# Softmax denominators of the first two attentions: key sums from three sources in one TensorE accumulation

## Chip, cores and metric

The kernel runs on one core of a Trainium2 chip. The metric is device time in microseconds (us) of one execution; the number to predict is the median over the timed runs of the changed kernel.

## The reference, cut to what matters

Three layers follow one another: an attention with capped scores, a dense feed-forward layer with squared ReLU, and a layer of eight experts with routing. The change touches only the sum of the exponentials over the keys, the denominator of the softmax, in the attention.

```python
def _attn_ref(q, k, v, cap):          # 4 batches, 12 heads, 448 tokens, head size 64
    scale = 1.0 / np.sqrt(q.shape[-1])
    scores = scale * np.matmul(q, k.transpose(0, 1, 3, 2))
    scores = cap * np.tanh(scores / cap)
    scores = scores - np.max(scores, axis=-1, keepdims=True)
    attn = np.exp(scores)
    attn = attn / (np.sum(attn, axis=-1, keepdims=True) + 1e-09)
    return np.matmul(attn, v).astype(np.float32)
def _moe_ref(x, w_in, w_out):         # 1792 x 768, width 2048
    h = x @ w_in
    r = np.maximum(h, 0.0)
    g = r * r
    return (g @ w_out).astype(np.float32)
...
```

The weights `w_in` and `w_out` arrive as 64-bit floating point numbers and are decoded on the chip; the kernel splits operands into a high and a low part to multiply at float32 accuracy.

## The kernel before, in words

Work is done batch by batch (b = 0 to 3). `attention(b)` handles the 12 heads as six pairs `hp` of two heads each. The 448 keys are cut into three chunks of 128 (c = 0, 1, 2) and a rest of 64. `scores(hp, c)` multiplies keys by queries for both heads of a pair (L239), the two heads standing side by side; for c = 3 the rests of both heads are packed into one tile, head 0 in rows 0 to 63 and head 1 in rows 64 to 127 (L241). ScalarE (ACT) then applies tanh (L243) and exp (L244), which gives the tiles `p` with keys on rows and queries on columns. `pv` multiplies them by the values into a tile `U` (L263). `norm(hp)` forms the denominators: the chunks have been added up elementwise in a tile `z`, and a matmul with a 128x64 block of ones sums over the 128 rows and spreads the sum over the 64 rows of each head (L269). Then L271 adds a small constant, L272 takes the reciprocal, and L274 multiplies `U` by it, which gives `x`.

The elementwise additions are: L250, chunk 0 plus chunk 1; L252, plus chunk 2; L256, twice, plus the packed rest, one half of the rows for each head. They run on VectorE (DVE) for b = 0 and on GpSimd (POOL) for b = 1 to 3.

```python
adder = nc.vector if b == 0 else nc.gpsimd
...
elif c == 2:
    adder.tensor_add(zs[hp], zs[hp], p)
elif c == KB:
    for s in range(2):
        half = slice(s * 64, s * 64 + 64)
        adder.tensor_add(zs[hp][half, s], zs[hp][half, s], p[half, 0])
```

`hidden(b)` is the first product of the feed-forward layer (L404 to L406, in the rows `acc<-xh,wh`, `acc<-xl,wh`, `acc<-xh,wl`), `output(b)` the second (L461 to L463, `acc<-g,...`). It needs all six `x` of its batch, split by L320 (ACT) and L321 (DVE). For b = 0 the weights are also decoded, on DVE (L333, L334, L335, tile `wf`), and split into a high part on ACT (L361) and a low part on DVE or POOL (L362); later batches read them back from a cache. `merge` interleaves the generators by the costs that they yield: `attention(0)` runs first alone, then `hidden(0)` with `attention(1)`, then `output(0)` and `hidden(1)` with `attention(2)`, and so on. Each engine has its own list of instructions and works through it in order; for b below 2 a scheduler chose that order, from b = 2 on TensorE's order is that of `merge`.

PSUM is held by three pools of two buffers each: `big` (scores), `acc` (feed-forward) and `aux` (`U` and `z` in turn). With two `aux` buffers, the next `U` takes the buffer of the last `z`, free after L271, and the next `z` takes that of the last `U`, free after L274. So the matmul of one `norm` waits for L274 of the `norm` before it.

Of the kernel before, what the change touches and what calls it, by code (L numbers as in the profile page):

```python
# [9 lines left out]
F32 = mybir.dt.float32  # L10
# [9 lines left out]
NB, NH, S, DH = 4, 12, 448, 64  # L20
# [7 lines left out]
KB = S // 128  # L28
# [16 lines left out]
AHEAD = 12  # L45
PLAIN = 4
EARLY = 6
WB = 4
START, MASK, VOTE, REST, GATHER, LIST = (7.7, 8.0), (1.85, 3.4), (1.0, 2.6), (0.86, 2.2), (11.0, 12.4), (6.0, 10.0)

# [35 lines left out]
class Kernel:  # L86
# [96 lines left out]
    def setup(self):  # L183
        nc, keep = self.nc, self.keep
        capt = keep.tile([128, 1], F32, name="capt")
        nc.sync.dma_start(capt, bass.AP(tensor=self.capv.tensor, offset=self.capv.offset, ap=[[0, 128], [1, 1]]))
        self.capt = capt
        self.ones = keep.tile([128, DH], F32, name="ones")
        nc.vector.memset(self.ones, 1.0)
        self.isc = keep.tile([128, 1], F32, name="isc")  # L190
        nc.vector.reciprocal(self.isc, capt)
        nc.vector.tensor_scalar(self.isc, self.isc, DH ** -0.5, None, op0=OP.mult)
        nab = keep.tile([128, 1], F32, name="nab")
        nc.vector.scalar_tensor_tensor(nab, capt, -1.0, capt, op0=OP.mult, op1=OP.min)
        self.eps = keep.tile([128, 1], F32, name="eps")
        nc.scalar.activation(self.eps, nab, AF.Exp)
        nc.vector.tensor_scalar(self.eps, self.eps, 1e-9, None, op0=OP.mult)
        self.L = keep.tile([128, TC, NE], F32, name="L")
        self.cache = {}
        self.wtile = {}  # L200
        self.seq, self.at = [], {}
        for b, m in ((0, "i"), (0, "o"), (1, "i"), (1, "o"), (2, "i"), (3, "i"), (3, "o"), (2, "o")):
            self.at[b, m] = len(self.seq)
            self.seq += [(b, m, j) for j in range(NF if m == "i" else ND * OB)]
        self.G = {}
        self.loaded = self.ready = 0
        self.x_t = {}
        self.tail = []
        self.exps, self.norms = [], []
        self.mark = None  # L210

    def attention(self, b):

        nc, ap = self.nc, self.ap
        qk, P, vt, zs, U = {}, {}, {}, {}, {}
        adder = nc.vector if b == 0 else nc.gpsimd

        def load(hp):
            qk[hp] = t = ap.tile([128, QK], F32, name="qk", bufs=2)
            if b + hp == 0:  # L220
                for half, q in ((0, nc.sync), (1, nc.scalar)):
                    q.dma_start(t[half * 64:half * 64 + 64], self.q_k[b, hp, half * 64:half * 64 + 64])
            else:
                nc.sync.dma_start(t, self.q_k[b, hp])

        def load_v(hp):
            vt[hp] = ap.tile([128, KB + 1, 2 * DH], F32, name="v", bufs=3)
            nc.sync.dma_start(vt[hp], self.v[b, hp])

        def scores(hp, c):  # L230

            t = qk[hp]
            n = 2 if c < KB else 1
            k, q = t[:, c * 128:(c + 1) * 128], t[:, QK - S:]
            ps = self.psum.tile([128, 2, 512], F32, name="big")
            if c < KB:
                for s in range(2):
                    rows = slice(s * 64, s * 64 + 64)
                    nc.tensor.matmul(ps[:, s, :S], k[rows], q[rows], start=True, stop=True)  # L239
            else:  # L240
                nc.tensor.matmul(ps[:, 0, :S], k, q, start=True, stop=True)  # L241
            p = ap.tile([128, n, S], F32, name=f"p{n}", bufs=(2, 5)[n - 1])
            nc.scalar.activation(p, ps[:, :n, :S], AF.Tanh, scale=self.isc)  # L243
            e = nc.scalar.activation(p, p, AF.Exp, scale=self.capt)  # L244
            if b == 0:
                self.exps.append(e)
            P[hp, c] = p
            if c == 1:
                zs[hp] = z = ap.tile([128, 2, S], F32, name="z", bufs=2)
                adder.tensor_add(z, P[hp, 0], p)  # L250
            elif c == 2:
                adder.tensor_add(zs[hp], zs[hp], p)  # L252
            elif c == KB:
                for s in range(2):
                    half = slice(s * 64, s * 64 + 64)
                    adder.tensor_add(zs[hp][half, s], zs[hp][half, s], p[half, 0])  # L256

        def pv(hp, c0, c1):
            if c0 == 0:
                U[hp] = self.psum.tile([128, S], F32, name="aux")  # L260
            for c in range(c0, c1):
                for s in range(2):
                    nc.tensor.matmul(U[hp][s * 64:s * 64 + 64], vt[hp][:, c, s * 64:s * 64 + 64], P[hp, c][:, s if c < KB else 0],  # L263
                                     start=(c == 0), stop=(c == KB), skip_group_check=True)

        def norm(hp):
            z = self.psum.tile([128, S], F32, name="aux")
            for s in range(2):
                nc.tensor.matmul(z[s * 64:s * 64 + 64], self.ones, zs[hp][:, s], start=True, stop=True)  # L269
            d = zs[hp][:, 0]  # L270
            (nc.vector.tensor_scalar(d, z, self.eps, None, op0=OP.add) if b == 0 else nc.scalar.activation(d, z, AF.Identity, bias=self.eps))  # L271
            nc.vector.reciprocal(d, d)  # L272
            x = self.xq.tile([128, S], F32, name="x")
            m = nc.vector.tensor_mul(x, U.pop(hp), d)  # L274
            if b == 0:
                self.norms.append(m)
            if b == NB - 1:
                self.mark = m
            self.x_t[b, hp] = x

        load(0)
        load(1)
        load_v(0)
        whole = b > 1
        for hp in range(HP + 1):
            if hp < HP:
                if hp + 1 < HP:
                    load_v(hp + 1)
                scores(hp, 0)
                if not whole:  # L290
                    yield 0.8
                scores(hp, 1)
                if not whole:
                    yield 0.8
            if hp:
                pv(hp - 1, 0, 2)
                if not whole:
                    yield 1.6
                pv(hp - 1, 2, 4)
                if not whole:  # L300
                    yield 1.6
                norm(hp - 1)
            if hp or whole:
                yield (4.4 if hp else 1.6) if whole else 0.8
            if hp < HP:
                scores(hp, 2)
                if not whole:
                    yield 0.8
                scores(hp, 3)
                if hp + 2 < HP:  # L310
                    load(hp + 2)
                yield 2.6 if whole else 0.6
# [28 lines left out]
    def load_weights(self, n):  # L341
# [5 lines left out]
        if b == 0:  # L347
            wf = self.wts.tile([128, DM], F32, name="wf", bufs=3)
            with self.after(self.norms, WAIT[0], n):
                self.decode(wf, (self.wi if m == "i" else self.wo)[j], w)  # L350
            self.wtile[n] = (wf, w, nc.gpsimd if n % 6 else nc.vector, self.wts, WB)
        else:
            self.wtile[n] = pair = [self.wts.tile([128, DM], F32R, name=name, bufs=WB) for name in ("wh", "wl")]
            for t, c in zip(pair, self.cache[m, j]):
# [463 lines left out]
    def load_experts(self, n):  # L818
        nc = self.nc
        while self.eloaded < min(n + 1 + AHEAD, len(self.eseq)) and self.eseq[self.eloaded][0] in self.full:  # L820
# [9 lines left out]
            plain = kk < PLAIN and mm == 1  # L830
            pool, bufs = (self.ep, 4) if self.esplit % 8 < 4 else (self.wts, WB)
            self.esplit += not plain
# [20 lines left out]
    def expert(self, k):  # L853
# [5 lines left out]
        def part(j, d0, d1):  # L859
            if d0 == 0:  # L860
                W[j] = [t.rearrange("p (d f) -> p d f", d=ND) for t in self.expert_weights(k, 1, j)]
                if k == 0 and 2 <= j < EARLY:
                    if j % 2 == 0:
# [27 lines left out]
        if k == 0:  # L891
            for i in range(EARLY):
                p = part(i, 0, DA)
# [8 lines left out]
        for group in groups:  # L902
            for j in group:
                yield from part(j, DA if k == 0 and j < EARLY else 0, ND)
            for j in group:
# [97 lines left out]
```

## Time and profile before

| what | value |
|---|---|
| median of three timed runs (lowest, highest) | 1053.39 us (1051.45, 1054.56) |
| the profiled execution's own time | 1056.75 us |
| its span, first to last instruction | 1055.0 us |
| TensorE (PE) busy | 1026.5 us, 97% |
| VectorE (DVE) busy | 602.5 us, 57% |
| ScalarE (ACT) busy | 468.1 us, 44% |
| GpSimd (POOL) busy | 244.7 us, 23% |

The busy share is a mean over stages that differ. VectorE is busy nearly all the time in the first 250 us (decoding of weights) and much less later, so the first quarter of the span has to be read by itself. A float32 matmul shows as two records in the trace, so a row "x4" of the attention's matmuls is two matmuls, one for each head of a pair.

### The profile page before, as it was taken

How to read it: one execution, taken by the hardware profiler on the slowest of the kernel's cores; microseconds unless marked ns; L12 is line 12 of the kernel's file. 1: busy time of each engine (PE TensorE's matmuls, PEld its weight loads, DVE VectorE, ACT ScalarE, POOL GpSimd, SP SyncE). 2: the span in 40 equal slices, each digit the busy share in tenths (PEclk: the TensorE clock that was granted, in tenths of full speed). 3: DMA queues.
4: the chain of work that ended last, by engine and by line, in shares of the span. 5: the costliest groups of instructions: out<-in, count | busy, mean ns of one | idle time of the engine just before them, and what ended most of it. 6: DMA issues, size and time to landing. Idle time of an engine off the chain costs nothing.

```text
span 1055.0 us, 15657 instructions
## 1 busy us (share of the span) xinstructions
PE 1026.5 (97%) x5690; PEld 815.2 (77%) x5690; DVE 602.5 (57%) x1148; ACT 468.1 (44%) x725; POOL 244.7 (23%) x181
## 2 busy tenths in 40 slices
PE   6989999999999999999999999999999999999997
PEld 1335665777677777777888788888899999999997
DVE  5997999999122255555411234534647348677552
ACT  5867686654465543365544110100323224445542
POOL 0117776665221222222000100001220201021000
PEclk9999999999999999999999999999999999999999
DMA  8653877899655579988687268667567358567530
GB/s 280 233 169 130 261 257 264 247 324 323 247 181 189 175 256 336 364 308 307 236 303 253 80 197 276 204 193 243 167 226 259 113 178 265 189 200 250 180 119 27
DMA packets 102494, 237.60 MB, mean 225 GB/s; under 512 B 11088, under 2 KB 21872, under 8 KB 102416
## 3 DMA queue, kind: packets, MB, share of 16 engines
q1 hardware_dynamic: 87776, 219.65, 61.5%
q0 software_dynamic: 3424, 11.19, 3.6%
q10 hardware_dynamic: 11216, 5.75, 2.0%
q8 instruction: 45, 0.74, 0.3%
q14 instruction: 33, 0.27, 0.1%
HBM read 194.08 MB, written 42.47 MB: 224 GB/s over the span
## 4 chain that ended last, share of the span: by engine, by line
PE 71%; issue 12%; DVE 10%; DMA 3%; ACT 1%; POOL 1%; SPq 0%; POOLq 0%; ACTq 0%; DVEq 0%
PE big L939 8%; PE acc L404 7%; PE acc L405 6%; PE acc L406 6%; PE acc L461 6%; PE acc L871 6%; PE acc L462 6%; PE acc L463 6%; PE aux L263 4%; PE big L239 3%; DVE wf L334 3%; DVE wf L333 2%; PE acc L878 2%; PE aux L676 2%; PE aux L269 1%
## 5 line engine op out<-in xcount | busy, mean ns | idle before, releaser
L461 PE MATMUL acc<-g,wh 128*128 128x448 f32 x384 | 149.5, 389 | 0.0
L404 PE MATMUL acc<-xh,wh 128*128 128x448 f32 x384 | 145.9, 382 | 0.7 <-ACT r L411 0.7
L405 PE MATMUL acc<-xl,wh 128*128 128x448 f32 x384 | 140.8, 367 | 0.9 <-DVE xl L321 0.9
L462 PE MATMUL acc<-g,wh 128*128 128x448 f32 x384 | 140.1, 365 | 0.0
L463 PE MATMUL acc<-g,wl 128*128 128x448 f32 x384 | 139.6, 364 | 0.0
L406 PE MATMUL acc<-xh,wl 128*128 128x448 f32 x384 | 139.5, 363 | 0.0
L939 PE MATMUL big<-wh,g 128*112 128x384 f32 x512 | 118.5, 343 | 0.0
L243 ACT ACTIVATE p<-big,isc 128x896 f32<-128x896 f32 x96 | 85.8, 908 | 43.3 <-PE big L239 43.3
L272 DVE RECIPROCAL z<-z 128x448 f32<-128x448 f32 x24 | 70.8, 2949 | 57.4 <-ACT z L271 57.4
L416 DVE TENSOR_TENSOR g<-r,g 128x448 fp32r<-128x448 f32 x58 | 42.7, 738 | 104.1 <-ACT g L415 103.8
L404 PEld LDWEIGHTS acc<-xh,wh 128*128 128x128 f32 x384 | 71.6, 187 | 34.3 <-issue 15.6
L244 ACT ACTIVATE p<-p,capt 128x896 f32<-128x896 f32 x96 | 89.4, 948 | 1.7
L783 POOL DMA_INDIRECT xg<-x,idx x32 | 31.6, 987 | 246.6 <-PE aux L676 129.4
L939 PEld LDWEIGHTS big<-wh,g 128*112 128x112 f32 x512 | 86.7, 175 | 0.7
L461 PEld LDWEIGHTS acc<-g,wh 128*128 128x128 f32 x384 | 73.2, 191 | 11.7 <-issue 5.6
L263 PE MATMUL aux<-p,v 128*64 128x448 f32 x384 | 81.1, 549 | 0.3 <-DVE z L271 0.3
L405 PEld LDWEIGHTS acc<-xl,wh 128*128 128x128 f32 x384 | 72.1, 188 | 9.9 <-issue 2.4
L239 PE MATMUL big<-qk 64*128 64x448 f32 x288 | 73.4, 600 | 6.5 <-DMA qk<-qk 6.2
L411 ACT ACTIVATE r<-acc 128x448 f32<-128x448 f32 x64 | 34.8, 543 | 99.1 <-PE acc L406 87.6
L462 PEld LDWEIGHTS acc<-g,wh 128*128 128x128 f32 x384 | 72.4, 189 | 6.3 <-issue 2.2
L463 PEld LDWEIGHTS acc<-g,wl 128*128 128x128 f32 x384 | 72.0, 187 | 6.7 <-issue 0.7
L406 PEld LDWEIGHTS acc<-xh,wl 128*128 128x128 f32 x384 | 72.0, 188 | 6.7 <-issue 0.8
(179 smaller groups left out, 1802.6 us busy)
## 6 DMA issues: line engine op xcount, KB each, us to landing
g<-w SPq DMA_DIRECT2D x62, 384.0 KB
wh<-wih SPq DMA_DIRECT2D x48, 384.0 KB
wl<-wil SPq DMA_DIRECT2D x48, 384.0 KB
wh<-woh SPq DMA_DIRECT2D x72, 256.0 KB
wl<-wol SPq DMA_DIRECT2D x72, 256.0 KB
wf<-w SPq DMA_DIRECT2D x33, 384.0 KB
raw<-w SPq DMA_DIRECT2D x33, 384.0 KB
raw<-w_in SPq DMA_DIRECT2D x16, 768.0 KB
```

Source lines behind the costliest of these rows:

```text
L239: nc.tensor.matmul(ps[:, s, :S], k[rows], q[rows], start=True, stop=True)
L243: nc.scalar.activation(p, ps[:, :n, :S], AF.Tanh, scale=self.isc)
L244: e = nc.scalar.activation(p, p, AF.Exp, scale=self.capt)
L263: nc.tensor.matmul(U[hp][s * 64:s * 64 + 64], vt[hp][:, c, s * 64:s * 64 + 64], P[hp, c][:, s if c < KB else 0], start=(c == 0), stop=(c = ...
L272: nc.vector.reciprocal(d, d)
L404: nc.tensor.matmul(ps, wh[:, d], xh, start=(d == 0), stop=False)
L405: nc.tensor.matmul(ps, wh[:, d], xl, start=False, stop=False)
L406: nc.tensor.matmul(ps, wl[:, d], xh, start=False, stop=(d == ND - 1))
L461: nc.tensor.matmul(ps, a, gh, start=(f == 0), stop=False)
L462: nc.tensor.matmul(ps, a, gl, start=False, stop=False)
L463: nc.tensor.matmul(ps, z, gh, start=False, stop=(f == NF - 1))
L939: nc.tensor.matmul(acc[h][:, s, :DM // 2], l, r[:, s * (DM // 2):(s + 1) * (DM // 2)], start=(j == 0 and first), stop=(j == NF2 - 1 and last))
```

## The change

For b = 0 and 1 only the first addition (chunk 0 plus chunk 1) is left as an elementwise operation, on DVE for b = 0 and on POOL for b = 1. `norm` then accumulates three sources in the same PSUM tile: the sum of the first two chunks with the weights of ones, the third chunk with the same weights, and the packed rest with new weights `pick`, a constant in which head s has ones in its own 64 rows and zeros in the others. Six matmuls stand where two stood. Three small fills of `pick` are added on POOL at the start. For b = 2 and 3 nothing is changed.

```diff
+DIRECT = 2
...
+        self.pick = keep.tile([128, 2, DH], F32, name="pick")
+        nc.gpsimd.memset(self.pick, 0.0)
+        for s in range(2):
+            nc.gpsimd.memset(self.pick[s * 64:s * 64 + 64, s], 1.0)
...
-        adder = nc.vector if b == 0 else nc.gpsimd
...
-                adder.tensor_add(z, P[hp, 0], p)
+                (nc.vector if b == 0 else nc.gpsimd).tensor_add(z, P[hp, 0], p)
+            elif b < DIRECT:
+                pass
             elif c == 2:
-                adder.tensor_add(zs[hp], zs[hp], p)
+                nc.gpsimd.tensor_add(zs[hp], zs[hp], p)
             elif c == KB:
                 for s in range(2):
                     half = slice(s * 64, s * 64 + 64)
-                    adder.tensor_add(zs[hp][half, s], zs[hp][half, s], p[half, 0])
+                    nc.gpsimd.tensor_add(zs[hp][half, s], zs[hp][half, s], p[half, 0])
...
-            for s in range(2):
-                nc.tensor.matmul(z[s * 64:s * 64 + 64], self.ones, zs[hp][:, s], start=True, stop=True)
+            parts = [zs[hp]] + ([P[hp, 2], P[hp, KB]] if b < DIRECT else [])
+            for i, p in enumerate(parts):
+                for s in range(2):
+                    w, r = (self.ones, p[:, s]) if i < 2 else (self.pick[:, s], p[:, 0])
+                    nc.tensor.matmul(z[s * 64:s * 64 + 64], w, r, start=i == 0, stop=i == len(parts) - 1, skip_group_check=True)
```

The scheduler orders the first two batches anew. Lines behind the edit have other numbers in the changed kernel: L239 becomes L243, L241 L245, L250 L254, L263 L269, L269 L278, L271 L280, L272 L281, L274 L283, L333 to L335 become L342 to L344, and L404 to L406 become L413 to L415.

On TensorE, the start of the program before (scores, values, and at the end the denominators of the first pair of heads):

```order
L241 MATMUL big<-qk 128x448
L263 MATMUL aux<-p_112,v 64x448 x2
L239 MATMUL big<-qk 128x448 x2
L263 MATMUL aux<-p_120,v 64x448 x2
L239 MATMUL big<-qk 128x448 x2
L263 MATMUL aux<-p_126,v 64x448 x2
L269 MATMUL aux<-z,ones 64x448 x2
```

And the same place now:

```order
L245 MATMUL big<-qk 128x448
L269 MATMUL aux<-p_116,v 64x448 x2
L278 MATMUL aux<-z,ones 64x448 x2
L243 MATMUL big<-qk 128x448 x2
L269 MATMUL aux<-p_124,v 64x448 x2
L278 MATMUL aux<-p_124,ones 64x448 x2
L243 MATMUL big<-qk 128x448 x2
L269 MATMUL aux<-p_129,v 64x448 x2
L278 MATMUL aux<-p_129,pick 64x448 x2
```

The first matmul of the denominators has moved ahead of the scores and values that stood before it; the two added ones follow the value matmuls that read the same tile.

On TensorE, one of the six `norm`s of `attention(1)`, which stand between the matmuls of `hidden(0)`, before:

```order
L405 MATMUL acc<-xl,wh 128x448
L406 MATMUL acc<-xh,wl 128x448
L269 MATMUL aux<-z,ones 64x448 x2
L404 MATMUL acc<-xh,wh 128x448
L405 MATMUL acc<-xl,wh 128x448
```

And now:

```order
L414 MATMUL acc<-xl,wh 128x448
L415 MATMUL acc<-xh,wl 128x448
L278 MATMUL aux<-z,ones 64x448 x2
L278 MATMUL aux<-p_662,ones 64x448 x2
L278 MATMUL aux<-p_682,pick 64x448 x2
L413 MATMUL acc<-xh,wh 128x448
L414 MATMUL acc<-xl,wh 128x448
```

Nothing else has moved there: the group of two matmuls has become a group of six. Behind the first matmuls of `output(0)`, TensorE's order is the same in both kernels.

On VectorE, the end of the first pair's `norm` in `attention(0)`, with the additions of the second pair (p_138 to p_174) between its steps, before:

```order
L271 TENSOR_SCALAR z<-aux,eps 128x448
L250 TENSOR_TENSOR z<-p_138,p_144 128x896
L272 RECIPROCAL z<-z 128x448
L252 TENSOR_TENSOR z<-z,p_168 128x896
L274 TENSOR_TENSOR x<-aux,z 128x448
L256 TENSOR_TENSOR z<-z,p_174 64x448 x2
L321 TENSOR_TENSOR xl<-x,xh 128x448
```

And now:

```order
L280 TENSOR_SCALAR z<-aux,eps 128x448
L254 TENSOR_TENSOR z<-p_139,p_145 128x896
L281 RECIPROCAL z<-z 128x448
L283 TENSOR_TENSOR x<-aux,z 128x448
L330 TENSOR_TENSOR xl<-x,xh 128x448
```

The two kinds of later additions are gone from between L271 and the split of `x`; the rest stands in the same order.

## Rows read from the trace of the kernel before

**Rows 1.** The page, busy us (share of the span) and instructions by engine.

```profile
PE 1026.5 (97%) x5690; PEld 815.2 (77%) x5690; DVE 602.5 (57%) x1148; ACT 468.1 (44%) x725; POOL 244.7 (23%) x181
```

**Rows 2.** Windows: busy us of each engine from 100 to 250 us.

```profile
core 0: us, PE busy (x) PEld busy (x) DVE busy (x) ACT busy (x) POOL busy (x), PEclk, DMA share, GB/s
100.00:250.00 150.00, 149.25 (x680) 99.71 (x678) 146.86 (x124) 95.26 (x144) 98.38 (x56) 1.00 0.81 265
```

**Rows 3.** Timeline of TensorE (start us, duration us, line): two records, 33 instructions of `hidden(0)` apart.

```profile
92.42 0.36 PE L406 MATMUL acc<-xh,wl 128*128 128x448 f32 x1
...
99.09 0.36 PE L406 MATMUL acc<-xh,wl 128*128 128x448 f32 x1
```

**Rows 4.** Waits of TensorE over the whole span: total us, times, longest.

```profile
PE big L239 <- DMA qk<-qk: 6.2, 1, 6.2
PE aux L269 <- DVE x L274: 4.3, 3, 2.2
PE aux L269 <- DVE z L256: 3.0, 1, 3.0
...
PE acc L405 <- DVE xl L321: 0.9, 2, 0.5
...
PE acc L404 <- ACT r L411: 0.7, 2, 0.4
...
PE aux L269 <- POOL z L256: 0.5, 1, 0.5
```

**Rows 5.** Timeline of TensorE around the last `norm` of `attention(0)`.

```profile
71.33 3.23 PE L263 MATMUL aux<-p,v 128*64 128x448 f32 x16
74.48 1.02 PE L239 MATMUL big<-qk 64*128 64x448 f32 x4
75.44 1.02 PE L241 MATMUL big<-qk 128*128 128x448 f32 x2
76.38 0.97 PE L269 MATMUL aux<-z,ones 128*64 128x448 f32 x4
77.29 0.67 PE L404 MATMUL acc<-xh,wh 128*128 128x448 f32 x2
```

**Rows 6.** Timeline of TensorE around the first `norm`.

```profile
12.80 0.97 PE L263 MATMUL aux<-p,v 128*64 128x448 f32 x4
13.70 1.02 PE L239 MATMUL big<-qk 64*128 64x448 f32 x4
...
20.43 2.41 PE L269 MATMUL aux<-z,ones 128*64 128x448 f32 x4 [2.96 <-DVE z L256]
22.77 1.84 PE L239 MATMUL big<-qk 64*128 64x448 f32 x4
24.54 1.02 PE L241 MATMUL big<-qk 128*128 128x448 f32 x2
```

**Rows 7.** Timeline of VectorE: the first addition.

```profile
14.67 1.10 DVE L250 TENSOR_TENSOR z<-p,p 128x896 f32<-128x896 f32 x1
```

**Rows 8.** Windows, columns as in rows 2: the granted clock (PEclk) after the wait.

```profile
22.00:24.00 2.00, 2.00 (x6) 0.51 (x4) 1.14 (x3) 0.00 (x0) 0.00 (x0) 0.50 0.81 216
```

**Rows 9.** Groups by line, VectorE, 0 to 100 us: count, busy us, mean ns.

```profile
L256 DVE TENSOR_TENSOR z<-z,p 64x448 f32<-64x448 f32 x12 | 9.8, 814 | 0.1
...
L252 DVE TENSOR_TENSOR z<-z,p 128x896 f32<-128x896 f32 x6 | 6.4, 1068 | 0.0
```

**Rows 10.** Groups by line, GpSimd, 100 to 250 us.

```profile
L256 POOL TENSOR_TENSOR z<-z,p 64x448 f32<-64x448 f32 x12 | 17.4, 1452 | 1.0 <-ACT p L244 0.4
...
L252 POOL TENSOR_TENSOR z<-z,p 128x896 f32<-128x896 f32 x7 | 16.0, 2282 | 16.9 <-ACT p L244 16.3 <-DVE wf L335 0.6
```

**Rows 11.** Timeline of GpSimd and VectorE: one operation of VectorE at two places.

```profile
126.39 2.14 POOL L362 TENSOR_TENSOR wl<-wf,wh 128x768 fp32r<-128x768 f32 x1
...
126.88 2.46 DVE L334 SCALAR_TENSOR_TENSOR wf<-raw,wf 128x768 int32<-128x768 int32 x1
...
131.38 0.96 DVE L334 SCALAR_TENSOR_TENSOR wf<-raw,wf 128x768 int32<-128x768 int32 x1
```

## Prediction

> **What bounds the kernel now.** The page's busy shares come first: TensorE 97%, VectorE 57% [rows 1]. Since VectorE is full early and idle late, the windows were read next for the stretch in which the first two attentions run beside the decoding. From 100 to 250 us both engines look full: TensorE is busy 149.25 of 150 us, VectorE 146.86 [rows 2]. The reader has to decide which of the two sets the pace there, because the change takes work from VectorE and GpSimd and gives some to TensorE.
>
> A busy TensorE need not be at its peak, as the ends of matmuls are modelled, so the third view is the timeline, read by starts. Between two records of `hidden(0)` that lie 33 instructions apart, 6.67 us pass [rows 3], 0.202 us each, and the starts between them are even: there is no slack between those matmuls. The fourth view is the list of TensorE's waits. Without the first load, which the change leaves alone, what it lists for the first 260 us is 4.3 us of L269 for L274 of the `norm` before, 3.0 us of L269 for the last addition L256, 0.9 for `xl`, 0.7 for `r` and 0.5 for an addition on GpSimd [rows 4]. The first three lie before 70 us. So TensorE waits some 9 us in the first 70 us, and hardly at all afterwards. VectorE in the second stretch is as full as TensorE, but TensorE does not stand still for it.
>
> **What the change adds.** Each of the 12 `norm`s gets two more pairs of matmuls. Sixteen records of value matmuls of the same shape (four pairs, weights of 128x64) take from 71.33 to 74.48, 3.15 us; the four records of one `norm` that stands alone take from 76.38 to 77.29, 0.91 us [rows 5]. The three pairs more cost 2.24 us, so 0.75 us a pair, and 0.16 us is the price of a break between matmuls of different shape. 24 pairs make 18.0 us. In `attention(1)` the six matmuls stand together where two stood, so no break is added. In `attention(0)` the new order has three more groups of values and denominators (3 x 0.16) and one fewer of scores, which costs 0.96 alone [rows 5], so 0.21 above 0.75: 0.3 us more. Together 18.3 us of TensorE, of which 9 lie in `attention(1)`, where TensorE shows no gap that could take them. No row shows the weights `pick`, but the value matmuls in the first row have their shape and change weights with every pair as well, so I take their price. If each added pair stood alone, at 0.91, it would be 21.8 us; 18.0 is the bound below. The three fills of `pick` run on GpSimd, beside the first load for which TensorE waits 6.2 us [rows 4]; without that cover they would delay only the first `pick` matmul.
>
> **What it removes.** On VectorE in `attention(0)`: six L252 of 1.07 us and twelve L256 of 0.81 us, 16.2 us, or 2.7 us a `norm` [rows 9]. On GpSimd in `attention(1)` six L252 and twelve L256. This is worth only what TensorE waited for it.
> - The first `norm`. TensorE was through its value matmuls and waited 2.96 us for L256, until 20.43 [rows 6]. Now its first matmul stands behind the second value group, where L239 started at 13.70 [rows 6]. It needs L250, which ends at 15.77 [rows 7], and nothing ahead of L250 on VectorE has gone. So TensorE waits 2.1 us there instead. Queued behind it are the scores of the second pair of heads, and ACT behind them; in the old kernel they waited later. Gain 0.85 us; bounds 0 and 2.96.
> - The clock. After the wait the granted clock was 0.50 [rows 8], the lower level of 1.2 GHz: the `norm` took from 20.43 to 22.77, 2.34 us instead of 0.91, and the scores behind it 1.77 instead of 0.96 [rows 5, 6], a loss of 2.24 us. The new wait is shorter, 2.1 us; whether the clock falls after it, no row shows. I take half, 1.1 us; bounds 0 and 2.24.
> - The waits for L274: 4.3 us in three, at most 2.2 each [rows 4]. In VectorE's new order the later additions are gone from the way from L271 to L274, and 2.7 us a `norm` is more than the longest. But each turn of `attention(0)` also gets shorter by its waits, and L280 can stand behind a decoding step or an L254 that waits for an exp. I take 3.8 us; bounds 0 and 4.3.
> - The waits for `xl` (0.9) and some of a few tenths for ACT and L271: 1.0 us; bounds 0 and 1.5.
> - After 70 us: 0.7 and 0.5 us [rows 4]. With less on GpSimd, VectorE gets ahead: 0.6 us; bounds 0 and 1.2.
>
> Sum of gains 7.35 us (bounds 0 and 12.2). Net 18.3 - 7.35 = 11 us longer; between 18.0 - 12.2 = 6 and, with nothing gained and each pair alone, 22. The profiled execution took 1056.75 us, so its counterpart should take 1067.7. The median of the runs before lies 3.4 us lower, at 1053.39, and the forecast for the median is 1064.4 us. Nothing behind 260 us takes the delay back: TensorE's order there is the same, and it was 97% busy over all [rows 1], so a shift has nowhere to go.
>
> **The rule that speaks for the change.** The Trainium skill, Perfetto Trace Analysis, section Identifying the Most-Contended Engine, says that matmul busy time is no good measure of TensorE's headroom, that the busy share of weight loads is, and that the engine with the highest occupancy is the one to relieve. Weight loads were busy 99.71 of 150 us and VectorE 98% [rows 2], so by this rule VectorE is the one to relieve and TensorE has room; the first rival below is what would follow. The even starts [rows 3] speak against it here.
>
> **The rivals.**
> - *VectorE sets the pace from 100 to 250 us, and the kernel gets faster.* For it: VectorE's 98%, and that its operations run longer beside GpSimd: the same L334 took 2.46 us when GpSimd was busy until 128.5, and 0.96 when it had nothing to do [rows 11], 0.6 us lost for each us of GpSimd. The additions removed from GpSimd after 100 us are five L252 of 2.28 and ten L256 of 1.45 us [rows 10], 26 us (the rest of the rows belongs to `attention(2)`), which frees up to 16 us of VectorE. If TensorE's work fitted into hidden gaps of this stretch, the time would fall by 16 us, less some 2 net in `attention(0)` (9.3 added, 6.75 gained): about 1040 us. It decides if TensorE's true gaps there reach 1.5 us for each `norm`. Against it: the starts, and 1.2 us of waits in all. The Trainium skill, SBUF — State Buffer, section SBUF: two separate sides, calls the port pair that VectorE and GpSimd share an exclusive lock; the two durations of L334 agree that the two engines hold each other up.
> - *The waits vanish and hidden ones with them, so nothing measurable is left.* To stay within 3.2 us (0.3%, about what a measurement of this kernel can tell from no change), 15 of the 18.3 us must come back. The listed waits and the lost clock give 12.2; the other 3 would have to be gaps too short for the list. That gives 1056 us.
> - *New waits in place of the old.* L280, which frees the PSUM buffer for the next `U`, now stands behind L254 in several turns, and L254 waits for the exp of the next pair of heads. If that held the value matmuls by 1 us in six of the turns, and the clock stayed down again after the first wait (1.1 us that I counted), the time would be 7 us more: 1071 us or above.
>
> **How the numbers follow.** My forecast, 1060 to 1070 us, gets 0.71; the new waits, above 1070, 0.13; no measurable change 0.09; faster 0.07. That makes slower 0.84. For 8 in 10 the range goes from 1058 us, just below what all waits gone would give (1053.4 + 6 = 1059.4), to 1071 us.
>
> **What would show it.** Right: the group of `norm` matmuls between those of `hidden(0)` takes 2.4 us instead of 0.9, with even starts before and after; the first `norm` waits about 2 us for L254 at about 13.7 us and is through near 22; TensorE's busy time and record count (96 more) grow; VectorE's busy time falls by 16 us and more and GpSimd's by some 30, with VectorE now idle in stretches between 100 and 250 us, which buys nothing. Wrong: matmuls of `hidden(0)` that start closer together or earlier than before, which would mean hidden gaps; a `norm` group that takes much less than 2.4 us; or the third and the packed source waiting for exp, which would add to the loss.

## The result, and the profile after

The changed kernel takes 1064.59 us (median; lowest 1063.67, highest 1065.23), the kernel before 1053.39 us. The ratio is 1.0102, with a 95% interval of 1.0086 to 1.0117: 10.7 us more, between 9.1 and 12.3 (ratio less 1, times 1053.4). It is slower by more than 0.3%, as forecast, and the forecast of 1064.4 us lies on the median.

The profiled execution after took 1063.67 us, only 6.9 more than the one before (1056.75), which lay 3.4 above its median; the prediction had 1067.7 for it. So the shift is better read inside the program, at work that the change leaves alone: the first and last transposes of the tile `lt` on TensorE. The rows are the answers for one source line, first of before, then of after; the two times behind the durations are the first and the last start.

```profile
L505 PE MATMUL aux<-cf,lt x14: 270/272/273, 290.1 to 605.1; 128*128 128x128 f32 x14
```

```profile
L514 PE MATMUL aux<-cf,lt x14: 270/273/273, 301.5 to 616.4; 128*128 128x128 f32 x14
```

The first starts 11.4 us later and the last 11.3 us later. All of the loss is made before the first of them, and in the 315 us between nothing is taken back.

The page's busy shares answer to [rows 1]: TensorE has 96 records and 13.7 us more, VectorE 35.1 us less, GpSimd 33.7 us less.

```profile
PE 1040.2 (98%) x5786; PEld 822.1 (77%) x5786; DVE 567.4 (53%) x1130; ACT 470.1 (44%) x725; POOL 211.0 (20%) x166
```

The windows of after, with the columns of [rows 2], show the stretch from 100 to 250 us and the two stretches after TensorE's longer waits. VectorE is now busy 121.00 of 150 us instead of 146.86, GpSimd 71.00 instead of 98.38, and TensorE is as full as before. The freed time has turned into idleness of the two. The clock of 1.00 from 16 to 18 us answers to the 0.50 of [rows 8].

```profile
16.00:18.00 2.00, 2.00 (x10) 0.64 (x12) 2.00 (x3) 0.05 (x1) 0.00 (x0) 1.00 0.80 329
60.00:64.00 4.00, 4.00 (x20) 1.16 (x20) 4.00 (x4) 1.40 (x3) 0.00 (x0) 1.00 0.72 232
100.00:250.00 150.00, 150.00 (x700) 97.05 (x699) 121.00 (x116) 94.48 (x139) 71.00 (x41) 1.00 0.74 247
```

TensorE's waits after, over the whole span, answer to [rows 4]. The waits for the last `norm`'s product (L274, now L283), for `xl` and for `r` are gone or nearly so; the 3.0 us for the last addition have become 1.9 us for the first (L254). New is a wait of 3.7 us in two for L280, which frees the PSUM buffer that the next `U` takes.

```profile
PE big L243 <- DMA qk<-qk: 6.5, 1, 6.5
PE aux L269 <- DVE z L280: 3.7, 2, 2.5
PE aux L278 <- DVE z L254: 1.9, 1, 1.9
PE aux L685 <- DVE mask L649: 0.6, 1, 0.6
PE aux L278 <- POOL z L262: 0.6, 1, 0.6
PE acc L880 <- ACT xs L816: 0.5, 1, 0.5
PE aux L696 <- DVE votes L693: 0.2, 1, 0.2
PE aux L278 <- DVE x L283: 0.2, 1, 0.2
```

TensorE's timeline after (start, duration, line) shows three places: the first `norm`, a stretch of `hidden(0)`, and a `norm` of `attention(1)`.

```profile
15.98 0.97 PE L278 MATMUL aux<-z,ones 128*64 128x448 f32 x4 [1.93 <-DVE z L254]
16.88 1.02 PE L243 MATMUL big<-qk 64*128 64x448 f32 x4
...
21.24 0.92 PE L278 MATMUL aux<-p,pick 128*64 128x448 f32 x4
22.09 1.02 PE L243 MATMUL big<-qk 64*128 64x448 f32 x4
...
95.23 0.36 PE L415 MATMUL acc<-xh,wl 128*128 128x448 f32 x1
...
101.90 0.37 PE L415 MATMUL acc<-xh,wl 128*128 128x448 f32 x1
...
133.78 0.37 PE L415 MATMUL acc<-xh,wl 128*128 128x448 f32 x1
134.07 0.97 PE L278 MATMUL aux<-z,ones 128*64 128x448 f32 x4
134.88 0.92 PE L278 MATMUL aux<-p,ones 128*64 128x448 f32 x4
135.63 0.92 PE L278 MATMUL aux<-p,pick 128*64 128x448 f32 x4
136.48 0.47 PE L413 MATMUL acc<-xh,wh 128*128 128x448 f32 x1
```

The first `norm` waits 1.93 us and goes on at full clock. The two records of `hidden(0)` lie 33 instructions and 6.67 us apart, exactly as in [rows 3], though VectorE is now far from full: there were no hidden gaps. The `norm` takes 136.48 - 134.07 = 2.41 us where two matmuls took 0.91, so (2.41 - 0.91) / 2 = 0.75 us for each added pair.

Where the new wait comes from shows in the timeline of all engines from 54 us on.

```profile
54.20 3.62 POOL L371 TENSOR_TENSOR wl<-wf,wh 128x768 fp32r<-128x768 f32 x2 [10.64 <-ACT wh L370]
...
56.07 2.16 DVE L342 TENSOR_SCALAR wf<-raw 128x768 int32<-128x768 int32 x1 [4.00 <-POOL wl L371]
...
58.26 0.96 DVE L343 SCALAR_TENSOR_TENSOR wf<-raw,wf 128x768 int32<-128x768 int32 x1
59.14 0.68 DVE L280 TENSOR_SCALAR z<-aux,eps 128x448 f32<-128x448 f32 x1
...
59.87 1.72 PE L269 MATMUL aux<-p,v 128*64 128x448 f32 x8 [2.52 <-DVE z L280]
61.52 0.65 PE L243 MATMUL big<-qk 64*128 64x448 f32 x2
```

VectorE, with its additions gone, stood idle for 4.00 us at a decoding step (L342) until GpSimd had finished a low part (L371) and with it the `wf` buffer. L280 stands behind two decoding steps, and TensorE's next value matmuls wait 2.52 us for L280.

The other of the two waits for L280, 1.17 us at 35.01 us, has no GpSimd in it:

```profile
30.78 0.96 DVE L371 TENSOR_TENSOR wl<-wf,wh 128x768 fp32r<-128x768 f32 x1 [2.08 <-ACT wh L370]
...
33.28 1.08 DVE L254 TENSOR_TENSOR z<-p,p 128x896 f32<-128x896 f32 x1
34.28 0.68 DVE L280 TENSOR_SCALAR z<-aux,eps 128x448 f32<-128x448 f32 x1
...
35.01 1.35 PE L269 MATMUL aux<-p,v 128*64 128x448 f32 x6 [1.17 <-DVE z L280]
```

There VectorE makes the low part itself, after 2.08 us of waiting for ScalarE's high part (L370), and L280 stands behind that, two decoding steps and L254.

### The profile page after: what moved, and what is told of

Read it like the earlier page. It is cut to its first block, busy times and chain, and to the rows that moved or that the text cites. A ratio compares the mean times of both kernels' runs of the same rounds, so it can differ in the third digit from the quotient of the medians.

```text
span 1061.7 us, 15799 instructions
## 1 busy us (share of the span) xinstructions
PE 1040.2 (98%) x5786; PEld 822.1 (77%) x5786; DVE 567.4 (53%) x1130; ACT 470.1 (44%) x725; POOL 211.0 (20%) x166
## 4 chain that ended last, share of the span: by engine, by line
PE 80%; issue 9%; DVE 6%; DMA 3%; ACT 1%; POOL 1%; SPq 0%; POOLq 0%; ACTq 0%; DVEq 0%
PE big L948 9%; PE acc L413 8%; PE acc L414 7%; PE acc L415 7%; PE acc L470 7%; PE acc L880 6%; PE acc L471 6%; PE acc L472 6%; PE aux L269 5%; PE big L243 4%; PE acc L887 3%; PE aux L278 3%; PE aux L685 2%; DVE wf L343 2%; PE big L245 1%
## 5 line engine op out<-in xcount | busy, mean ns | idle before, releaser
L413 PE MATMUL acc<-xh,wh 128*128 128x448 f32 x384 | 146.8, 384 | 0.0
L415 PE MATMUL acc<-xh,wl 128*128 128x448 f32 x384 | 140.0, 365 | 0.0
L281 DVE RECIPROCAL z<-z 128x448 f32<-128x448 f32 x24 | 70.8, 2949 | 66.2 <-ACT z L280 66.1
L413 PEld LDWEIGHTS acc<-xh,wh 128*128 128x128 f32 x384 | 71.8, 188 | 33.4 <-issue 17.9
L425 DVE TENSOR_TENSOR g<-r,g 128x448 fp32r<-128x448 f32 x58 | 38.2, 660 | 110.7 <-ACT g L424 110.4
L269 PE MATMUL aux<-p,v 128*64 128x448 f32 x384 | 84.5, 551 | 3.7 <-DVE z L280 3.7
L470 PEld LDWEIGHTS acc<-g,wh 128*128 128x128 f32 x384 | 73.3, 191 | 12.2 <-issue 6.3
L243 PE MATMUL big<-qk 64*128 64x448 f32 x288 | 72.3, 593 | 6.5 <-DMA qk<-qk 6.5
L371 POOL TENSOR_TENSOR wl<-wf,wh 128x512 fp32r<-128x512 f32 (+1 forms) x33 | 54.4, 1653 | 121.1 <-ACT wh L370 109.9
L342 DVE TENSOR_SCALAR wf<-raw 128x512 int32<-128x512 int32 (+1 forms) x64 | 46.2, 739 | 59.8 <-DMA raw<-w_out_t 29.7
L415 PEld LDWEIGHTS acc<-xh,wl 128*128 128x128 f32 x384 | 72.1, 188 | 6.9 <-issue 1.0
```

Source lines behind the costliest of these rows:

```text
L413: nc.tensor.matmul(ps, wh[:, d], xh, start=(d == 0), stop=False)
L415: nc.tensor.matmul(ps, wl[:, d], xh, start=False, stop=(d == ND - 1))
L470: nc.tensor.matmul(ps, a, gh, start=(f == 0), stop=False)
```

## The experiments

Two theories stand against each other. **A**: TensorE sets the pace from the start to `output(0)`; the time is that of the added matmuls less the waits of TensorE that go, and relief of VectorE and GpSimd is worth those waits alone. **B**: VectorE and GpSimd set the pace from 100 to 250 us; relieving them gives time there that the added matmuls use up. The table holds every run; "us" is (ratio - 1) x 1053.4, and the last column the shift of the first `lt` transpose against 290.1 us. The kernel before had medians from 1053.4 to 1057.6 us beside these runs, so only ratios are compared. The scheduler orders every edit anew, so each run changes TensorE's order too, and no run holds it fixed. The shifts, from one execution each, follow the times within 2.5 us; verdicts go by the times.

| run | ratio (95%) | us | shift |
|---|---|---|---|
| after | 1.0102 (1.0086 to 1.0117) | +10.7 | +11.4 |
| e1_b0_only | 1.0056 (1.0042 to 1.0069) | +5.9 | +7.3 |
| e2_b1_only | 1.0068 (1.0054 to 1.0082) | +7.2 | +7.5 |
| e3_relief_only | 0.9941 (0.9927 to 0.9955) | -6.2 | -7.0 |
| e4_matmuls_only | 1.0148 (1.0132 to 1.0163) | +15.6 | +17.3 |
| e5_low_on_dve | 1.0088 (1.0070 to 1.0107) | +9.3 | +9.7 |
| e6_first_pair | 0.9998 (0.9987 to 1.0009) | -0.2 | +2.3 |
| e7_b0_adds_on_gpsimd | 1.0029 (1.0017 to 1.0040) | +3.1 | +2.9 |
| e8_first_pair_rest_gpsimd | 1.0016 (1.0003 to 1.0029) | +1.7 | +2.1 |
| e9_packed_only | 0.9962 (0.9949 to 0.9976) | -4.0 | -4.4 |
| e10_three_pairs | 0.9980 (0.9971 to 0.9989) | -2.1 | +0.1 |
| e11_packed_both | 0.9986 (0.9976 to 0.9995) | -1.5 | +0.6 |
| e12_packed_first | 0.9968 (0.9956 to 0.9980) | -3.4 | -2.4 |

**The change in the first attention alone** (against the changed kernel):

```diff
-DIRECT = 2
+DIRECT = 1
```

> The change for b = 0 alone; attention(1) keeps its additions on GpSimd. Theory A (TensorE sets the pace; the change costs its added matmuls less the waits that it removes): 9.3 us added, some 6.5 us of waits and lost clock gained, so +2 to +4 us against the kernel before. Theory B (VectorE sets the pace from 100 to 250 us): nothing is changed there, 16 us of VectorE are gone before, so 0 to -7 us.

It cost 5.9 us, more than the 2 to 4 expected. TensorE's window from 60 to 64 us and its timeline there say why.

```profile
60.00:64.00 4.00, 4.00 (x14) 1.13 (x12) 4.00 (x4) 0.01 (x1) 0.00 (x0) 0.60 0.80 248
```

```profile
59.62 3.12 PE L269 MATMUL aux<-p,v 128*64 128x448 f32 x8 [2.51 <-DVE z L280]
62.67 1.28 PE L243 MATMUL big<-qk 64*128 64x448 f32 x4
```

The wait for L280 is the same as in the changed kernel (2.51 against 2.52 us), but here the granted clock fell to 0.60, and the eight records behind it took 62.67 - 59.62 = 3.05 us instead of 61.52 - 59.87 = 1.65. The forecast's 9.3 us for this part, less the waits and the clock that went (12.2 us before; here 6.9 us of waits for L280, L254, L262 and L283 and some 1.6 us of clock are left), make 5.6 us. How much clock is lost differs between executions of this one kernel: the fastest (1058.09 us) shows a mean granted clock of 0.998, the other four, at 1059.53 to 1060.66 us, 0.995 to 0.996.

**The change in the second attention alone** (against the changed kernel; `norm` has the same condition, and the additions of the first attention are all on VectorE again):

```diff
-            elif b < DIRECT:
+            elif b == 1:
                 pass
             elif c == 2:
-                nc.gpsimd.tensor_add(zs[hp], zs[hp], p)
+                (nc.vector if b == 0 else nc.gpsimd).tensor_add(zs[hp], zs[hp], p)
```

> The change for b = 1 alone; attention(0) keeps its additions on VectorE. Theory A: six norms with 1.5 us more each and nearly no wait to remove, +8 to +9 us against the kernel before. Theory B: GpSimd's relief frees up to 14 us of VectorE, so the time falls, by 5 to 14 us.

It cost 7.2 us. This speaks most directly on theory B, since VectorE was relieved in the stretch in question and nothing else was: the window shows it busy 123.61 us where it was 146.86 [rows 2].

```profile
100.00:250.00 150.00, 150.00 (x695) 98.71 (x693) 123.61 (x116) 92.22 (x138) 70.73 (x42) 1.00 0.76 251
```

23 us less on VectorE and 28 less on GpSimd bought little more than the waits of 0.7 and 0.5 us [rows 4]: 12 x 0.75 = 9.0 us added, less 1.2, is 7.8. The shift of 7.5 us also holds some 1.5 us of clock, lost in a stretch that the edit leaves alone: behind a wait of 2.19 us for L283 the granted clock fell to 0.50, where the kernel before kept 1.00 behind its own 2.19 us (for L274).

```profile
70.00:72.00 2.00, 2.00 (x7) 1.37 (x8) 2.00 (x1) 1.97 (x3) 0.00 (x0) 0.50 0.27 104
```

So up to 1.8 us of the profiled execution came back beyond the list. Counted by TensorE's starts up to the first `lt` transpose, with waits left out, scores and feed-forward take some 1.4 us less in this run's order (an estimate); that covers most of it, and theory B asks for a time that falls by 5 to 14 us.

**The additions left out and no matmul added** (against the changed kernel), and **the matmuls added and the additions kept** (against the kernel before):

```diff
-            parts = [zs[hp]] + ([P[hp, 2], P[hp, KB]] if b < DIRECT else [])
+            parts = [zs[hp]]
```

```diff
+        self.zero = keep.tile([128, DH], F32, name="zero")
+        nc.gpsimd.memset(self.zero, 0.0)
...
-            for s in range(2):
-                nc.tensor.matmul(z[s * 64:s * 64 + 64], self.ones, zs[hp][:, s], start=True, stop=True)
+            parts = [zs[hp]] + ([P[hp, 2], P[hp, KB]] if b < 2 else [])
+            for i, p in enumerate(parts):
+                for s in range(2):
+                    w, r = (self.zero if i else self.ones, p[:, s if i < 2 else 0])
+                    nc.tensor.matmul(z[s * 64:s * 64 + 64], w, r, start=i == 0, stop=i == len(parts) - 1, skip_group_check=True)
```

> The later additions of b = 0 and 1 are left out and no matmul is added: the denominators of these two batches lack the third chunk and the rest. Theory A: only waits and the lost clock go, -6 to -9 us against the kernel before, and 17 to 19 us below the changed kernel. Theory B: VectorE's 16 us and up to 14 us by contention go, -16 to -30 us.

> The additions stay as before, and the matmuls of the change are added with weights of zero, so that nothing is relieved. Theory A: +18 us against the kernel before, less what the waits of attention(0) take in (each turn of VectorE stays as long while TensorE has 1.5 us more to do in it): +13 to +18 us. Theory B: the 9 us in attention(1) are hidden behind VectorE, so +9 us or less.

Relief without a price is worth 6.2 us, and the price without relief is 15.6 us (18.0 by the forecast's row). Both fall where theory A has them and outside what theory B asks. Together they make 9.4 us, within the 9.1 to 12.3 of the change. In the run with relief alone VectorE is nearly as idle as after (window below), and still the gain stays under the 9.2 us of waits and clock that went (12.2, less 3.0 for L254 that are left); part of the 3 us that don't show lies in TensorE's order, which breaks values and denominators into more and smaller groups there (some 1.3 us more by their starts); the rest is open.

```profile
100.00:250.00 150.00, 150.00 (x688) 97.66 (x687) 124.38 (x119) 95.41 (x143) 79.98 (x46) 1.00 0.79 261
```

With the additions kept, the first wait stays and so does the fall of the clock, and now the four added matmuls (eight records) fall under it. TensorE's timeline of that run:

```profile
20.89 2.41 PE L274 MATMUL aux<-z,ones 128*64 128x448 f32 x4 [3.39 <-DVE z L258]
22.44 3.85 PE L274 MATMUL aux<-p,zero 128*64 128x448 f32 x8
26.22 1.39 PE L241 MATMUL big<-qk 64*128 64x448 f32 x4
```

The `norm` takes 26.22 - 20.89 = 5.33 us, at a granted clock of 0.50 (the lower level, 1.2 GHz) from 22 to 26 us, against 2.41 us at full clock.

**The new wait's cause: the first low parts on VectorE** (against the changed kernel; GpSimd then has nothing to hold L342 up with):

```diff
-            self.wtile[n] = (wf, w, nc.gpsimd if n % 6 else nc.vector, self.wts, WB)
+            self.wtile[n] = (wf, w, nc.gpsimd if n > 3 and n % 6 else nc.vector, self.wts, WB)
```

> The changed kernel, with the low parts of the first four weight tiles made on VectorE instead of GpSimd. In the changed kernel TensorE waits 3.7 us for L280, which is late behind a decoding step that waits for GpSimd's low parts. Theory A, with that as the cause: most of the 3.7 us goes, -2 to -4 us against the changed kernel, so +7 to +9 against the kernel before. If L280 is late by the order of VectorE's list whatever GpSimd does: no change, +11.

The two waits for L280 in this run:

```profile
34.81 1.72 PE L269 MATMUL aux<-p,v 128*64 128x448 f32 x8 [1.12 <-DVE z L280]
...
57.60 1.72 PE L269 MATMUL aux<-p,v 128*64 128x448 f32 x8 [0.44 <-DVE z L280]
```

The long wait fell from 2.52 to 0.44 us and the short one stayed, so the total fell from 3.7 to 1.6 us, and the `lt` transposes start 1.7 us earlier than after (299.8 against 301.5). The time points the same way (9.3 us against 10.7, where 7 to 9 were expected), but the two intervals overlap, so it is the trace that shows it. GpSimd's low parts were the larger part of the long wait; the rest, 1.6 us, stays with VectorE's own order.

**Only the first pair of heads**, and **the first pair with the other additions of b = 0 on GpSimd** (against the changed kernel; the first with the additions of the other pairs on VectorE, as in e2), and **no matmul at all, but the later additions of b = 0 on GpSimd** (against the kernel before):

```diff
-            elif b < DIRECT:
+            elif b + hp == 0:
                 pass
```

```diff
             elif c == 2:
-                adder.tensor_add(zs[hp], zs[hp], p)
+                nc.gpsimd.tensor_add(zs[hp], zs[hp], p)
```

> The change for the first pair of heads of b = 0 alone. Theory A: 1.5 us of matmuls added, against a wait shorter by 1 us and 0 to 2.2 us of lost clock that come back; the waits for L274 stay: -2 to +1 us against the kernel before. Theory B: 2.7 us of VectorE's work less, long before 100 us, so 0 to -3 us; this run does not tell the two apart and is there as a candidate for a faster kernel.

> The kernel before, with L252 and L256 of b = 0 on GpSimd, which is idle for most of the first 70 us; no matmul added. Theory A: VectorE is relieved of 16 us there, but a GpSimd addition takes 2.2 us (two halves 2.9) and holds up VectorE beside it; if the relief counts, the waits for L274 go and the time falls by 2 to 5 us; the first norm waits longer, for GpSimd. If contention eats the relief: 0 to +3 us.

> The first pair of heads of b = 0 as in the change, the later additions of the other five pairs on GpSimd. Theory A: the gain of both runs before together, without the long wait of the first norm: -3 to -7 us against the kernel before; with contention as strong as after 100 us, -2 to +1.

One pair alone moves the first wait and leaves the others: 4.4 us for L283 in three, 2.5 us for L254, and no measurable change. The clock did not come back here either:

```profile
15.84 1.02 PE L278 MATMUL aux<-z,ones 128*64 128x448 f32 x4 [2.54 <-DVE z L254]
```

```profile
18.00:20.00 2.00, 2.00 (x6) 0.53 (x6) 1.82 (x2) 1.27 (x2) 0.00 (x0) 0.50 0.53 111
```

Behind the 2.54 us at the first `norm` the granted clock fell to 0.50, as it did in the kernel before behind 2.96. GpSimd is no cheaper place for the additions: 3.1 and 1.7 us more. The waits of the first of these two (e7) over the whole span:

```profile
PE aux L263 <- DVE z L271: 6.2, 3, 5.0
PE aux L269 <- POOL z L256: 3.2, 2, 2.3
```

The wait for L274 is down to 0.2 us as hoped, but L271 comes late, by 5.0 us once, and the granted clock is 0.85 from 60 to 80 us. The expected gain of the second (e8) fell the same way: 6.3 us for L280.

**Only the packed rest by `pick`, for b = 0** (against the changed kernel; the third chunk stays on VectorE and b = 1 as before), and **three of the six pairs** (`norm` has the same condition, and the other additions of b = 0 are on VectorE):

```diff
-            elif b < DIRECT:
-                pass
             elif c == 2:
-                nc.gpsimd.tensor_add(zs[hp], zs[hp], p)
-            elif c == KB:
+                (nc.vector if b == 0 else nc.gpsimd).tensor_add(zs[hp], zs[hp], p)
+            elif c == KB and b:
...
-            parts = [zs[hp]] + ([P[hp, 2], P[hp, KB]] if b < DIRECT else [])
+            parts = [zs[hp]] + ([P[hp, KB]] if b == 0 else [])
...
-                    w, r = (self.ones, p[:, s]) if i < 2 else (self.pick[:, s], p[:, 0])
+                    w, r = (self.ones, p[:, s]) if i < 1 else (self.pick[:, s], p[:, 0])
```

```diff
-DIRECT = 2
+DIRECT = (0, 3, 4)
...
-            elif b < DIRECT:
+            elif b == 0 and hp in DIRECT:
```

> For b = 0 only the packed rest goes through the new weights (one pair of matmuls more for each of six norms); the third chunk stays with VectorE's L252, and b = 1 is as in the kernel before. Theory A: 4.5 us of TensorE added, 9.8 us of VectorE gone; the first norm waits less for VectorE, the waits for L274 shrink: gains of 4 to 6 us, so -2 to +1 us against the kernel before. Theory B: nothing changes from 100 us on, 0 to -4 us.

> The change for the pairs 0, 3 and 4 of b = 0 alone, the pairs whose norms wait or make the next one wait most. Theory A: 4.5 us added; the first wait shrinks by 1 us, the lost clock may come back (0 to 2.2), two of the waits for L274 (3.8 us) go in part: -2 to +2 us against the kernel before. If new waits for L280 come up as in the changed kernel: +2 to +5 us.

The packed rest alone makes the kernel faster than both: 0.9962 (0.9949 to 0.9976), 4.0 us, more than the 2 that theory A allowed. Its waits over the span, and the window that answers to [rows 2]:

```profile
PE big L243 <- DMA qk<-qk: 6.4, 1, 6.4
PE aux L276 <- DVE z L256: 2.4, 1, 2.4
...
PE aux L267 <- DVE z L278: 1.5, 1, 1.5
PE aux L276 <- DVE x L281: 0.8, 1, 0.8
```

```profile
100.00:250.00 150.00, 150.00 (x688) 100.11 (x689) 147.28 (x123) 96.11 (x144) 104.20 (x59) 1.00 0.84 272
```

Six pairs cost 6 x 0.75 = 4.5 us and take two VectorE instructions of 0.81 us [rows 9] out of each `norm`, where the third chunk's pair costs the same 0.75 and takes out only one of 1.07 us. Of the 12.2 us of waits and clock 4.7 are left, so 7.5 come back, and 4.5 - 7.5 = -3.0 us. VectorE stays as full as before from 100 to 250 us: this gain lies in the first 70 us. The last `hidden(0)` matmul with `acc<-xh,wh` starts 3.0 us earlier than before (175.6 against 178.6). The other 1.4 us of the shift of 4.4 arise at a `norm` of `attention(2)`, which the edit doesn't touch. In the kernel before its two heads' matmuls stood apart, the second behind a wait for GpSimd; here they ran together (first row before, second row this run):

```profile
255.66 0.97 PE L269 MATMUL aux<-z,ones 128*64 128x448 f32 x2 [0.51 <-POOL z L256]
```

```profile
251.26 0.92 PE L276 MATMUL aux<-z,ones 128*64 128x448 f32 x4
```

Whether that holds in the other executions, no trace shows. Half the pairs of the original form give 2.1 us, although the clock fell there as in e6 (a wait of 2.51 us at the first `norm`, 0.50 from 18 to 20 us).

**The packed rest in both attentions**, and **with the third chunk of the first pair as well** (against e9's kernel):

```diff
-            elif c == KB and b:
+            elif c == KB and b >= DIRECT:
...
-            parts = [zs[hp]] + ([P[hp, KB]] if b == 0 else [])
+            parts = [zs[hp]] + ([P[hp, KB]] if b < DIRECT else [])
```

```diff
+            elif b + hp == 0:
+                pass
             elif c == 2:
...
-            parts = [zs[hp]] + ([P[hp, KB]] if b == 0 else [])
+            parts = [zs[hp]] + ([P[hp, 2]] if b + hp == 0 else []) + ([P[hp, KB]] if b == 0 else [])
...
-                    w, r = (self.ones, p[:, s]) if i < 1 else (self.pick[:, s], p[:, 0])
+                    w, r = (self.ones, p[:, s]) if i == 0 or p is P[hp, 2] else (self.pick[:, s], p[:, 0])
```

> The packed rest by the new weights in b = 0 and in b = 1, the third chunk by additions in both. The run with b = 0 alone took 0.9962 of the kernel before, 4 us less. Theory A: six more pairs in attention(1), where TensorE has no gap, cost 4.5 us and give back less than 1: about the time of the kernel before, -1 to +1 us. Theory B: 17 us of GpSimd's work less beside VectorE's decoding make it faster than with b = 0 alone: -6 us or better.

> The packed rest of b = 0 by the new weights, and for the first pair of heads the third chunk as well. Theory A: 0.75 us more of TensorE; in the run with the packed rest alone the first norm still waited 2.4 us for VectorE's L252, and 2 us of wait for L250 take its place, so -4.5 to -3 us against the kernel before, no clear difference from that run.

The same edit that gains in the first attention loses in the second: from 0.9962 to 0.9986, some 2.5 us (the intervals just meet at 0.9976), and the shift of the `lt` transposes grows by 5.0 us (4.5 by six pairs), while VectorE was freed of 13 us and GpSimd of 21:

```profile
100.00:250.00 150.00, 149.99 (x690) 100.04 (x691) 134.09 (x119) 93.27 (x138) 83.56 (x47) 1.00 0.79 258
```

One more pair for the first `norm` makes no difference that can be told from e9.

## Why the prediction was right, point by point

**The bound.** TensorE set the pace from 100 to 250 us, as the prediction read from the even starts [rows 3]. Shown by e2, e3 and e11: VectorE relieved by 23, 22 and 13 us in that stretch, with at most some 2 us gained beyond the listed waits. The first rival, which had 16 us, is refuted. With it falls, for this kernel, the rule of the Trainium skill, Perfetto Trace Analysis, section Identifying the Most-Contended Engine, which pointed at VectorE; the measurement decides. In that rival one price was read too low: the L334 of [rows 11] lost 1.5 us beside a GpSimd operation of 2.14 us, 0.7 us for each rather than 0.6; that changes neither the sum nor the forecast.

**The price.** 0.75 us for a pair, from the value matmuls [rows 5], held to the hundredth in `attention(1)` (2.41 us for a `norm`, 2.4 forecast). The price of `pick` is that of the ones.

**The gains.** The net time came out as forecast, but the sum of the gains and several of its terms did not:

| term | forecast, us | trace after against [rows 4, 6] |
|---|---|---|
| wait of the first `norm` | -0.85 | 2.96 to 1.93: -1.0 |
| clock behind it | -1.1 | 2.24 lost before, nothing after: -2.2 |
| waits for L274 | -3.8 | 4.3 to 0.2: -4.1 |
| `xl` and small ones | -1.0 | 0.9, 0.3 and 0.3 gone: -1.5 |
| after 70 us | -0.6 | 0.7 gone, 0.5 to 0.6: -0.6 |
| new waits for L280 | none | +3.7 |
| first load | none | 6.2 to 6.5: +0.3 |
| sum | -7.35 | -5.4 |

With 18.3 us added the listed terms give 12.9 us, the shift is 11.4 and the time 10.7; the missing 1.5 us have no row. Counted by TensorE's starts up to the first `lt` transpose (a gap beyond the usual one between the same two kinds of matmul counts as a wait), values and denominators take 17.9 us more, waits, lost clock and first load together 4.7 less, and all other matmuls 1.8 less; these are estimates. So the missing part lies in the new order of scores and feed-forward, for which the prediction had no term. The forecast's hit is in part luck: a smaller gain from the waits and a cheaper order cancel.

Besides that, two steps were wrong. One is the clock ("I take half"): all of it came back in the profiled execution, and in e5 and e9, whose waits there are 1.96 and 2.39 us. In e6 and e10, whose waits there are 2.54 and 2.51 us, it fell. The other four executions of the changed kernel show a mean granted clock of 0.997 to 0.998 against 0.999 and took 0.9 to 1.6 us longer, so some clock may be lost in them; no trace shows where. The other step is the wait for L280, which the prediction had only as its third rival, put down to an L254 that waits for an exp. It came at two places and with another cause: 2.52 us behind a decoding step that waits for GpSimd, which e5 shows by taking most of it away, and 1.17 us behind L254, but with no wait for an exp. The third rival's other half, a clock that stays down after the first wait, did not come in the changed kernel; it came in e6 and e10, and in e1 at the later wait.

**What would show it.** The 96 records, the `norm` of 2.4 us, the first `norm` waiting 1.93 us for L254 (2.1 forecast; it was through at 22.09, 22 forecast), VectorE and GpSimd freed of 35 and 34 us and idle for it: all are there.

What stays open is why the clock fell after a wait of 2.51 us in e1 and not after one of 2.52 us at the same place in the changed kernel. The executions of one kernel differ in their mean clock as well, so one trace of each can't settle it.

## What to carry to other kernels

Two engines that are both 98 to 99% busy are told apart by the starts: if the busier one's instructions follow each other evenly and its list of waits is short, relief of the other is worth about that list (here within some 2 us). Price each piece of moved work against the wait that it removes, stage by stage: the packed rest in the first attention paid 4.5 us for some 7.5 us of waits and gained, and the same edit in the second, where hardly anything waits, only cost. Moving work also gives the scheduler another order, and here that moved the time by 1 to 2 us, either way (an estimate from the starts). When a full engine is relieved, look for what it will now wait on: here VectorE ran into GpSimd at one place and into its own list at another, and 3.7 of the 9.4 us gained went into the new wait.

## What the runs showed of the hardware

- Waits of the same length differ in what the granted clock does behind them: 0.60 from 60 to 64 us in e1 after 2.51 us, 1.00 in the changed kernel after 2.52 us. After 2.19 us at the third wait for L283 it fell to 0.50 in e2 and stayed at 1.00 in the kernel before. At the first `norm`, after 3.0 us (before, e2), 3.39 (e4), 2.54 (e6) and 2.51 (e10) the matmuls behind ran at half speed; after 1.93 (after) and 2.39 us (e9) they did not.
- The decoding step L342 took 2.16 us, from 56.07 on, while GpSimd worked until 54.20 + 3.62 = 57.82 us, and 0.55 at 61.60 with GpSimd idle, like L334 in [rows 11]. Moving some 16 us of additions to GpSimd (e7) made the kernel 3.1 us slower rather than faster.
